# Attention into SwiGLU: how normalised x of batches 1 to 7 reaches its transposed ring

## The chip, the core and the metric

The kernel runs on one core of a Trainium2 chip. The metric is device time in microseconds (us). A core has engines that each run their own instruction stream in order and wait for one another by semaphores: TensorE (PE, with its weight loads PEld), VectorE (DVE), ScalarE (ACT), GpSimd (POOL), and SyncE (SP), which here does nothing but issue DMAs. The DMAs of all queues are carried out by 16 DMA engines of the core. TensorE reads SBUF and writes PSUM; DVE and ACT bring results from PSUM back to SBUF.

## The reference

Causal attention with a decay bias (8 batches, 8 heads, 576 positions, 64 dims a head), whose output is read as 4608 tokens of 512 values and put through an RMS norm and a SwiGLU layer:

```python
scores = q @ k.T / sqrt(D)                       # per batch and head
bias = -(cum[..., :, None] - cum[..., None, :])  # cum = cumsum(max(s, 0))
attn = softmax(where(causal, -1e9, scores + minimum(bias, 0)))
x = (attn @ v).transpose(0, 2, 1, 3).reshape(B * S, H * D)
xn = x / sqrt(mean(x * x, -1) + 1e-6) * rms_g
g = xn @ w_gate
out = (g * sigmoid(g) * (xn @ w_val)) @ w_out    # w_gate, w_val 512x1536, w_out 1536x512
```

## The kernel before, in words

Both halves are woven into one instruction stream per engine. The layer (`ffn(c)`, L464) works on nine chunks c of 512 tokens: twelve times four gate matmuls (L472) and four value matmuls (L481) of 128x512, with tanh on ACT (L475) and two products on DVE (L484, L477), then four groups of twelve output matmuls (L496), each drained by ACT into `osb` (L501) and stored by SP (L503). `osb` has three buffers.

Attention works on batches of 576 tokens in five blocks `qb` (four of 128 rows and one of 64). Its pieces are: T, transposing k and q on TensorE (L146) with copies by ACT (L154) or DVE (L152); S, the scores (L196) with exponentials on ACT (L212) and the causal mask on POOL (L218); AV, the product with v (L233, L239), whose result DVE divides into `x_sb` (L246, L248). After the second AV of a block DVE squares x (L253), POOL makes 1/rms from the sum (L256, L259), and DVE scales x into `xs_sb` (`x_scale`, L266). `x_sb` and `xs_sb` have four buffers (NX). XT (`xt_step`, L270) then takes the block to the ring `xnT`, in which a token is a column: four TensorE transposes of 128x128 into PSUM (L274, tile `psT`, a single buffer that T uses too) and one DVE copy into `xnT` (L279; a second one, L281, where the block wraps round the end). The ring holds 2048 tokens, four chunks. It is read by L472 and L481.

k and q of a batch come as float32 by SP (`load_kq`, L117, 1 MB each; tails L123, 128 KB each) into a single buffer `kq32`; POOL casts them (L133) in ten pieces. The load of batch b+1 waits until the casts of batch b have read the buffer, so it is issued after the last of them. v is loaded by POOL (L137). DVE also runs range checks on k and q (L284, L290).

The order is set at build time by a planner in the code. `step()` (L424) counts one slot; `ffn` calls it 36 times in a chunk, and `need(c)` (L453) calls it until the last block of chunk c has its XT. In each slot `step` issues at most one scale, one side job (POOL casts, v loads or a DVE check), and then either one S or up to two of XT, AV and T. An AV may be placed only when the XT of the block four before it is `done` (L410 to L412, since its buffers are the same); T and XT must be two slots apart from each other (`last["T"]`, L384 and L416); S must be two or three slots apart. A block's scale is placed 3 slots after its second AV, its XT 6 slots after it or later. Casts of a batch wait until 9 slots after its load was placed. Batch 0 (blocks 0 to 3) is written out by hand ahead of chunk 0 (L633 to L686). The tile framework adds the semaphores; SP's stream has stores, loads and whatever else is issued there in the order in which the code places them.

Of the kernel before, what the change touches and what calls it, by code (L numbers as in the profile page):

```python
# [26 lines left out]
def kernel(  # L27
# [12 lines left out]
    nc = tc.nc  # L40
    B, H, S, D = q.shape
# [5 lines left out]
    NSC = 5  # L47
# [4 lines left out]
    RING = 4 * DM  # L52

    def rows(c):
        return 128 if c < 4 else 64
# [18 lines left out]
    xnT = mp.tile([128, CC, RING], BF16, name="xnT")  # L74
# [8 lines left out]
    NX = 4  # L83
    x_sb = mp.tile([128, NX, DM], BF16, name="x_sb")
    xs_sb = mp.tile([128, NX, DM], BF16, name="xs_sb")
# [22 lines left out]
    def psT():  # L108
        return pp.tile([128, 8, 128], BF16, name="psT", tag="T", bufs=1)
# [5 lines left out]
    def load_kq(eng, b, w, h0=0, h1=H):  # L115
        src = k if w == 0 else q
        eng.dma_start(  # L117
            out=kq32[:, w, h0:h1, 0:256],
            in_=src[b, h0:h1, 0:512, :].rearrange("h (p r) d -> p h (r d)", r=4))

    def load_kq_tail(eng, b, w):
        src = k if w == 0 else q
        eng.dma_start(  # L123
            out=kq32[0:64, w, :, 256:320],
            in_=src[b, :, 512:576, :].rearrange("h p d -> p h d"))

    def cast(eng, b, w, r0, r1, h0=0, h1=H):
        o = kqn[:, b % 2, w, r0:r1, h0:h1, :]
        i = kq32[:, w].rearrange("p h (r d) -> p r h d", d=D)[:, r0:r1, h0:h1, :]
        if eng is nc.scalar:  # L130
            eng.activation(out=o, in_=i, func=AF.Copy)
        else:
            eng.tensor_copy(out=o, in_=i)  # L133
# [129 lines left out]
    def x_scale(b, qb):  # L263
        n = rows(qb)
        col = b * NSC + qb
        nc.vector.tensor_scalar(  # L266
            out=xs_sb[0:n, (b * NSC + qb) % NX, :], in0=x_sb[0:n, (b * NSC + qb) % NX, :],
            scalar1=al_all[0:n, col:col + 1], scalar2=None, op0=ALU.mult)

    def xt_step(b, qb):  # L270
        n = rows(qb)
        pX = psT()
        for cc in range(CC):
            nc.tensor.matmul(pX[:, cc, :], lhsT=xs_sb[:, (b * NSC + qb) % NX, cc * 128:(cc + 1) * 128],  # L274
                             rhs=ident_bf, is_transpose=True,
                             start=(cc == 0), stop=(cc == CC - 1))
        t0 = (b * S + qb * 128) % RING
        m = min(n, RING - t0)
        nc.vector.tensor_copy(out=xnT[:, :, t0:t0 + m], in_=pX[:, 0:CC, 0:m])  # L279
        if m < n:  # L280
            nc.vector.tensor_copy(out=xnT[:, :, 0:n - m], in_=pX[:, 0:CC, m:n])  # L281
# [14 lines left out]
    slot = [0]  # L296
    done = {}
# [3 lines left out]
    xt_seq = [(b, qb) for b in range(B) for qb in range(NSC)]  # L301
    t_seq = [(b, hp, w) for b in range(B) for hp in list(range(HP)) + ["tail"]
             for w in (0, 1) if hp != "tail" or w == 0]
    pending = []
    pool_side, dve_side, v_side = [], [], []

    def at(*key):
        return done.get(key, 10 ** 6)

    def ready(lag, *key):  # L310
        return at(*key) + lag <= slot[0]

    def run_side(queue):
        if queue and queue[0][0]():
            queue.pop(0)[1]()

    def later(queue, lag, fns):
        t = slot[0] + lag
        queue.extend((lambda: slot[0] >= t, f) for f in fns)

    def check(b):
        later(dve_side, 2, [f for w in (0, 1) for f in (
            lambda w=w: check_mag(b, w), lambda: check_max(0), lambda: check_max(1))]
            + [lambda: done.__setitem__(("check", b), slot[0])])

    def casts(b):

        def over():
            done["cast", b] = slot[0]
            if b + 1 < B:  # L330
                for w in (0, 1):
                    load_kq(nc.sync, b + 1, w)
                    load_kq_tail(nc.sync, b + 1, w)
                done["raw", b + 1] = slot[0]
            check(b)
        fns = [lambda w=w, r=r: cast(nc.gpsimd, b, w, r, r + 1) for w in (0, 1) for r in range(NSC)]
        pool_side.extend((lambda: ready(9, "raw", b) and ready(0, "check", b - 2), f)
                         for f in fns + [over])
# [10 lines left out]
    def do_t(key, **kw):  # L349
        b, hp, w = key  # L350
        if hp == "tail":
            tail_step(b)
            done["T", b] = slot[0]
            after_tail(b)
        else:
            t_step(b, hp, w, **kw)
        done["T", b, hp, w] = slot[0]
        last["T"] = slot[0]

    def do_s(key, pair=None):  # L360
        b, kb, g = key
        second = s_step(b, kb, g, pair)
        done["S", b, kb, g] = slot[0]
        if kb == 4:
            done["S", b, 4, 1] = slot[0]
        last["S"] = slot[0]
        return second

    def do_av(key):
        b, qb, g = key  # L370
        av_step(b, qb, g)
        done["AV", b, qb, g] = slot[0]
        last["AV"] = slot[0]
        if qb == 4 and g == 1:
            after_av(b)

    def do_xt(key):
        b, qb = key
        xt_step(b, qb)
        done["XT", b, qb] = slot[0]  # L380
        last["T"] = slot[0]

    def can_t():
        if not t_seq or slot[0] - last["T"] < 2:  # L384
            return False
        b, hp, w = t_seq[0]
        return ready(2, "cast", b) and (b < 2 or ready(1, "S", b - 2, 4, 0))

    def can_s():
        if not s_seq or not slot_free():  # L390
            return False
        b, kb, g = s_seq[0]
        due = SLOTS * ((b * S + kb * 128) // DM) - 14
        if slot[0] - last["S"] < (3 if slot[0] < due else 2):
            return False
        if kb >= 3 and not ready(3, "T", b):
            return False
        if kb == 4:
            return True
        return all(ready(3, "T", b, 2 * g + j, w) for j in (0, 1) for w in (0, 1))  # L400

    def can_av():
        if not av_seq or slot[0] - last["AV"] < 2:
            return False
        b, qb, g = av_seq[0]
        if b > 1 and not ready(8, "V", b):
            return False
        if qb > 0 and not ready(5, "S", b, qb - 1, g):
            return False
        prev = b * NSC + qb - NX  # L410
        if prev >= 0 and at("XT", prev // NSC, prev % NSC) > slot[0]:
            return False  # L412
        return ready(5, "S", b, qb, g)

    def can_xt():
        if not xt_seq or slot[0] - last["T"] < 2:  # L416
            return False
        b, qb = xt_seq[0]
        return ready(6, "AV", b, qb, 1)

    scaled = [0]
    x_list = [(b, qb) for b in range(B) for qb in range(NSC)]
# [1 line left out]
    def step():  # L424

        slot[0] += 1
        while pending:
            pending.pop(0)()
        if scaled[0] < len(x_list):
            b, qb = x_list[scaled[0]]  # L430
            if ready(3, "AV", b, qb, 1):
                x_scale(b, qb)
                scaled[0] += 1
        if v_side and slot[0] % 2:
            run_side(v_side)
        else:
            run_side(pool_side)
        if slot[0] % 2:
            run_side(dve_side)
        if can_s():  # L440
            pending.append(do_s(s_seq.pop(0)))
            return
        n = 0
        if can_xt():
            do_xt(xt_seq.pop(0))
            n += 1
        if can_av():
            do_av(av_seq.pop(0))
            n += 1
        if n < 2 and can_t():  # L450
            do_t(t_seq.pop(0))

    def need(c):  # L453

        lastt = (c + 1) * DM - 1
        key = (lastt // S, (lastt % S) // 128)
        n = 0
        while at("XT", *key) > slot[0]:
            step()
            n += 1  # L460
            assert n < 200, key
# [428 lines left out]
```

## Time and profile before

| | us |
|---|---|
| time, median of 3 runs (lowest to highest) | 421.24 (421.04 to 421.57) |
| the profiled execution: its time | 420.97 |
| the profiled execution: span from first to last instruction | 419.4 |
| mean granted TensorE clock | 0.992 |
| ACT busy, share of the span | 217.8 (52%) |
| POOL busy, share of the span | 180.1 (43%) |
| first gate matmul of chunks 0 to 4, from the span's start | 47.17, 100.57, 144.47, 189.41, 229.33 |
| the same of chunks 5 to 8 | 270.76, 311.05, 349.58, 381.62 |

The page gives each engine's busy time, the span in forty slices, the DMA queues, the chain that ended last, and groups of instructions with their mean duration and the idle time before them. L12 is line 12 of the kernel. In a timeline a line gives start, duration, engine, line, operation and count; matmuls are pipelined, so the duration of one is longer than the time by which it moves the next, and costs on TensorE are read from the distance of starts.

### The profile page before, as it was taken

What the parts mean: (1) busy time and instruction counts of PE and PEld (TensorE: products, weight loads), DVE (VectorE), ACT (ScalarE), POOL (GpSimd) and SP (SyncE); (2) the same over time, 40 slices, a digit from 0 to 9 for tenths busy, and PEclk for the clock granted to TensorE, in tenths of its full rate; (3) what the DMA queues carried; (4) which work ended last, traced back from release to release, by engine and by line L of the source; (5) the groups of instructions that cost most, each with busy time, mean ns of one, the idle gap of its engine ahead of it and who ended that gap; (6) DMA issues with size and microseconds to landing.
All of it is one profiled execution on the core that took longest, in us unless ns stands there. A gap on an engine that the chain in (4) does not pass through costs nothing. (4 is left out here: it accounts for less than half of the span.)

```text
span 419.4 us, 7416 instructions
## 1 busy us (share of the span) xinstructions
PE 371.8 (89%) x2679; PEld 183.2 (44%) x2679; DVE 322.2 (77%) x678; ACT 217.8 (52%) x516; POOL 180.1 (43%) x288
## 2 busy tenths in 40 slices
PE   1563779698999889999999999999999999999993
PEld 1342433344544444445445444444454445444441
DVE  4458499899899699988897899979767966764740
ACT  2661265652577647644765486558645753323321
POOL 6767727576717757535734575343221320000000
PEclk9999999899999999999999999999999999999998
DMA  9999985348931755629242630190020011001002
GB/s 241 215 232 256 178 135 36 22 135 211 150 115 50 233 70 50 208 79 81 76 153 76 64 21 25 65 69 2 27 76 2 2 50 52 1 29 73 1 28 80
DMA packets 72125, 38.46 MB, mean 92 GB/s; under 512 B 47440, under 2 KB 67408, under 8 KB 72080
## 3 DMA queue, kind: packets, MB, share of 16 engines
q0 software_dynamic: 41168, 9.44, 24.4%
q1 hardware_dynamic: 29776, 27.27, 20.9%
q10 hardware_dynamic: 1136, 1.20, 0.8%
q8 instruction: 23, 0.38, 0.4%
q14 instruction: 22, 0.18, 0.1%
HBM read 37.90 MB, written 9.44 MB: 113 GB/s over the span
## 5 line engine op out<-in xcount | busy, mean ns | idle before, releaser
L212 ACT ACTIVATE E<-psS,biasK 128x256 bf16<-128x256 f32 (+2 forms) x300 | 105.6, 434 | 33.3 <-PE psS L196 30.6
L472 PE MATMUL psF<-xnT,wg_sb 128*128 128x512 bf16 x432 | 111.9, 382 | 2.0 <-DVE xnT L279 1.1
L481 PE MATMUL psF<-xnT,wv_sb 128*128 128x512 bf16 x432 | 112.8, 384 | 0.5 <-DVE Ht L477 0.2
L496 PE MATMUL psF<-wout_sb,Ht 128*128 128x512 bf16 x432 | 104.9, 379 | 0.0
L475 ACT ACTIVATE T<-psF 128x512 f32<-128x512 f32 x108 | 64.7, 599 | 74.3 <-PE psF L472 62.8
L218 POOL TENSOR_SCALAR_AFFINE_SELECT E<-E 128x512 bf16<-128x512 bf16 x72 | 49.5, 688 | 99.9 <-ACT E L212 98.9
L484 DVE SCALAR_TENSOR_TENSOR U<-T,psF 128x512 bf16<-128x512 f32 x108 | 73.7, 683 | 18.3 <-ACT T L475 17.9
L477 DVE TENSOR_TENSOR Ht<-U,psF 128x512 bf16<-128x512 bf16 x99 | 67.5, 682 | 5.5 <-PE psT L146 0.5
L481 PEld LDWEIGHTS <-wv_sb 128*128 128x128 bf16 x432 | 39.3, 98 | 45.4 <-issue 6.9
L472 PEld LDWEIGHTS <-wg_sb 128*128 128x128 bf16 x432 | 38.1, 98 | 39.0 <-issue 7.2
L496 PEld LDWEIGHTS <-Ht 128*128 128x128 bf16 x432 | 37.8, 98 | 38.0 <-issue 2.7
L133 POOL CAST kqn<-kq 128x512 bf16<-128x512 f32 (+1 forms) x80 | 51.7, 669 | 4.0 <-DMA kq<-in_k_dram 2.3
L501 ACT ACTIVATE osb<-psF 128x512 f32<-128x512 f32 x36 | 21.6, 601 | 48.6 <-PE psF L496 45.0
L256 POOL TENSOR_SCALAR al_all<-ss_all 128x1 f32<-128x1 f32 (+1 forms) x40 | 15.9, 397 | 62.8 <-DVE xs_sb L253 62.2
L248 DVE TENSOR_TENSOR x_sb<-psAV,rZ 128x256 bf16<-128x256 f32 (+1 forms) x80 | 33.8, 423 | 2.7
L239 PE MATMUL psAV<-v_sb,E 128*128 128x65 bf16 x320 | 30.2, 199 | 5.9 <-POOL E L218 5.9
L137 POOL DMA_DIRECT2D v_sb<-in_v_dram x40 | 35.3, 889 | 0.0
L233 PE MATMUL psAV<-v_sb,E 128*128 128x65 bf16 x256 | 25.7, 198 | 6.9 <-DVE x_sb L248 6.9
L196 PE MATMUL psS<-kqT 64*128 64x256 bf16 (+2 forms) x300 | 25.7, 257 | 6.3 <-ACT E L212 4.9
L253 DVE SCALAR_TENSOR_TENSOR xs_sb<-x_sb 128x512 bf16<-128x512 bf16 (+1 forms) x40 | 29.7, 743 | 1.4
L154 ACT ACTIVATE kqT<-psT 128x512 bf16<-128x512 bf16 x32 | 19.4, 607 | 19.9 <-PE psT L146 19.9
L239 PEld LDWEIGHTS <-E 128*128 128x128 bf16 x320 | 22.8, 101 | 14.3 <-POOL E L218 6.4
(82 smaller groups left out, 318.2 us busy)
## 6 DMA issues: line engine op xcount, KB each, us to landing
out_dram<-osb SPq DMA_DIRECT2D x36, 256.0 KB, 2.0
kq<-in_k_dram SPq DMA_DIRECT2D x7, 1024.0 KB, 5.9
kq<-in_q_dram SPq DMA_DIRECT2D x7, 1024.0 KB, 6.7
v_sb<-in_v_dram POOLq DMA_DIRECT2D x32, 128.0 KB, 4.4
wg_sb<-in_moe_w_gate_dram POOLq DMA_DIRECT2D x2, 768.0 KB, 15.0
wv_sb<-in_moe_w_val_dram POOLq DMA_DIRECT2D x2, 768.0 KB, 19.5
wout_sb<-in_moe_w_out_dram POOLq DMA_DIRECT2D x1, 1536.0 KB, 14.7
kq<-in_k_dram SPq DMA_DIRECT2D x2, 512.0 KB, 5.2
```

The source lines that it names most:

```text
L133: eng.tensor_copy(out=o, in_=i)
L137: nc.gpsimd.dma_start(out=v_sb[0:n, b % 2, c, :, 0:64], in_=v[b, :, c * 128:c * 128 + n, :].rearrange("h p d -> p h d"))
L212: nc.scalar.activation(out=Ev[:, h - h0, 0:N], in_=pair[par][:, o:o + N], func=AF.Exp, scale=0.125, bias=biasK[:, kb, bh:bh + 1])
L218: nc.gpsimd.affine_select(out=Ev[:, :, 0:nq], in_=Ev[:, :, 0:nq], pattern=[[0, nh], [1, nq]], compare_op=ALU.is_ge, fill=0.0, base=0, chan ...
L239: nc.tensor.matmul(o, lhsT=d, rhs=v_sb[:, p, qb, h, :], start=(j == 0 and qb == 0), stop=(j == 3))
L248: nc.vector.tensor_tensor(out=xo[:, g * 256:(g + 1) * 256].rearrange("p (h d) -> p h d", h=4), in0=pv[0:n, :, 0:64], in1=rZ[0:n].unsqueeze ...
L472: nc.tensor.matmul(Gp, lhsT=wg_sb[:, cc, fs], rhs=xnT[:, cc, x0:x0 + DM], start=(cc == 0), stop=(cc == CC - 1))
L475: nc.scalar.activation(out=T, in_=Gp, func=AF.Tanh, scale=0.5)
L477: nc.vector.tensor_tensor(out=Ht[:, fb - 1, :], in0=pend[0], in1=pend[1], op=ALU.mult)
L481: nc.tensor.matmul(Vp, lhsT=wv_sb[:, cc, fs], rhs=xnT[:, cc, x0:x0 + DM], start=(cc == 0), stop=(cc == CC - 1))
L484: nc.vector.scalar_tensor_tensor(out=U, in0=T, scalar=1.0, in1=Gp, op0=ALU.add, op1=ALU.mult)
L496: nc.tensor.matmul(Op, lhsT=Ht[:, fb, tb * 128:(tb + 1) * 128], rhs=wout_sb[:, fb, :], start=(fb == 0), stop=(fb == FB - 1))
```

## The change

Blocks of batches 1 to 7 no longer take XT. Where the planner places a block's scale, it now also places a transposing DMA on SP's queue that reads `xs_sb` and writes the block's columns of `xnT` (two DMAs where the block wraps round), and declares the block's XT done four slots later. `can_xt` lets only batch 0 through. The loads of k and q for the next batch, so far placed right behind the last cast, are placed by a new side list three slots later.

```diff
+    def xt_dma(b, qb):
+        n = rows(qb)
+        t0 = (b * S + qb * 128) % RING
+        m = min(n, RING - t0)
+        i = (b * NSC + qb) % NX
+        nc.sync.dma_start_transpose(out=xnT[:, :, t0:t0 + m], in_=xs_sb[0:m, i, :])
+        if m < n:
+            nc.sync.dma_start_transpose(out=xnT[:, :, 0:n - m], in_=xs_sb[m:n, i, :])
...
             done["cast", b] = slot[0]
             if b + 1 < B:
-                for w in (0, 1):
-                    load_kq(nc.sync, b + 1, w)
-                    load_kq_tail(nc.sync, b + 1, w)
-                done["raw", b + 1] = slot[0]
+                def loads():
+                    for w in (0, 1):
+                        load_kq(nc.sync, b + 1, w)
+                        load_kq_tail(nc.sync, b + 1, w)
+                    done["raw", b + 1] = slot[0]
+                later(sp_side, 3, [loads])
...
-        return ready(6, "AV", b, qb, 1)
+        return b == 0 and ready(6, "AV", b, qb, 1)
...
                 x_scale(b, qb)
                 scaled[0] += 1
+                if b > 0:
+                    assert xt_seq[0] == (b, qb)
+                    xt_dma(*xt_seq.pop(0))
+                    done["XT", b, qb] = slot[0] + 4
+        run_side(sp_side)
```

More of the change, by code (lines that the diff above doesn't have):

```diff
@@ L304 @@
     pending = []
-    pool_side, dve_side, v_side = [], [], []
+    pool_side, dve_side, v_side, sp_side = [], [], [], []
     def at(*key):
```

## The prediction, made before the changed kernel was run

> **What bounds the kernel now.** I read the page first. TensorE is busy 89% of the span, DVE 77%; from slice 6 on TensorE's row is almost all nines, with the clock at full.
>
> ```profile
> PE 371.8 (89%) x2679; PEld 183.2 (44%) x2679; DVE 322.2 (77%) x678; ACT 217.8 (52%) x516; POOL 180.1 (43%) x288
> PE   1563779698999889999999999999999999999993
> DVE  4458499899899699988897899979767966764740
> ```
>
> Shares over the whole span mix stages, so next comes the table by chunk (stretch; its length; busy us of PE, PEld, DVE, ACT, POOL; clock; DMA share; GB/s). I cut it at the chunk starts.
>
> ```profile
> 100.60:144.50 43.90, 41.33 (x317) 20.68 (x317) 36.67 (x69) 28.25 (x67) 26.46 (x41) 1.00 0.57 119
> 144.50:189.40 44.90, 42.22 (x340) 20.92 (x340) 42.27 (x92) 25.18 (x62) 25.09 (x38) 1.00 0.52 113
> 189.40:229.30 39.90, 39.90 (x309) 19.59 (x307) 34.72 (x72) 24.66 (x61) 21.07 (x34) 1.00 0.51 101
> 229.30:270.80 41.50, 40.94 (x329) 20.19 (x327) 36.70 (x78) 25.31 (x62) 20.90 (x34) 1.00 0.30 41
> 270.80:311.00 40.20, 40.20 (x319) 19.88 (x317) 30.54 (x70) 25.32 (x61) 13.60 (x24) 1.00 0.30 42
> 349.60:381.60 32.00, 31.63 (x153) 14.34 (x150) 21.09 (x34) 10.03 (x17) 0.72 (x2) 1.00 0.09 34
> ```
>
> From chunk 1 TensorE has no more than 2.7 us of gaps in a chunk. Chunk 7, almost without attention, takes 32.0 us; the 8 to 13 us that chunks 1 to 5 take beyond that are attention's TensorE work. So TensorE's own sequence sets the time; in chunk 2 DVE (42.27 of 44.9) is close behind. Last, the timeline around one XT:
>
> ```profile
> 192.22 1.03 PE L481 MATMUL psF<-xnT,wv_sb 128*128 128x512 bf16 x4
> 193.08 0.39 PE L274 MATMUL psT<-ident_bf,xs_sb 128*128 128x128 bf16 x4
> 193.31 1.03 PE L472 MATMUL psF<-xnT,wg_sb 128*128 128x512 bf16 x4
> ```
>
> By starts, four long matmuls take 0.86 us (192.22 to 193.08) and the four transposes 0.23 (to 193.31). The page's 230 ns for one transpose is its pipelined length, not its price.
>
> **Removed.** 35 blocks (seven batches of five) lose XT. TensorE: 35 x 0.23 = 8.05 us, all on the path. Four of them (batch 1, blocks 0 to 3) precede chunk 1, whose start will be set by a DMA (below), so I count 31 x 0.23 = **-7.1 us**. DVE: the copies sum to 15.35 us (L279) and 0.56 (L281), less batch 0's 1.96: 13.9 us, beside TensorE's work except where TensorE waits for them. Those waits on the path are at the start of chunk 2, 0.50 for `psT` and 0.44 for the ring after 1.09 for scores. By the planner's rules they change: the block that chunk 2 needs last (batch 2, block 2) has AV, scale and XT at slots 70, 73, 76, and three slots in `need` go without layer matmuls; with T no longer kept two slots from XT, that AV comes at 66, the scale and its DMA at 69, and chunk 2 starts at 74 with no extra slot. I take **-1.5** (bounds 0 and -2.0).
>
> **Added.** 35 transposing DMAs of 128 KB (two blocks in halves). SP's issue costs it 0.33 to 0.8 us a DMA by the rows of L503 and L123; SP has the time, and no engine waits for the issue. No row shows how long a transposing DMA takes. The nearest rows (KB, then us from issue to landing):
>
> ```profile
> out_dram<-osb SPq DMA_DIRECT2D x36, 256.0 KB, 2.0
> kq<-in_k_dram SPq DMA_DIRECT2D x7, 1024.0 KB, 5.9
> v_sb<-in_v_dram POOLq DMA_DIRECT2D x32, 128.0 KB, 4.4
> kq<-in_q_dram SPq DMA_DIRECT2D x8, 128.0 KB, 6.8
> ```
>
> Below stands 2.0 (long rows, twice the bytes), above 6.8 (same bytes, but queued behind megabytes). I take **4.4**: the same bytes in short runs, as a block is written to 128 partitions in 256-byte runs. The Trainium skill, "VectorE: DVE Perf Modes", section "The three transpose paths", gives 1309 ns for a 128x128 bf16 transpose by DMA against 390 on TensorE, and advises TensorE where PSUM will do. Four of those in a row would be an estimated 5.2 us a block, and the sum by it about 417 (0.8 later at chunk 1, 0.2 at chunk 2); no run here shows it yet.
>
> Where is it late? A block of chunk 3 or later is scaled 11 slots or more ahead of its chunk (batch 3 block 2 at slot 99, chunk 3 at 110; batch 4 block 1 at 122, chunk 4 at 146), at about 1.13 us a slot (40.5 us a chunk over 36). Chunk 2's has five slots, 5.7 us: enough for 4.4. Chunk 1's (batch 1, block 3) is scaled at slot 34, and chunk 1 begins at 38. The trace there:
>
> ```profile
> 93.72 5.87 SPq L503 DMA_DIRECT2D out_dram<-osb  x3
> 96.29 0.33 DVE L266 TENSOR_SCALAR xs_sb<-x_sb,al_all 128x512 bf16<-128x512 bf16 x1
> 100.11 0.41 DVE L279 COPY xnT<-psT 128x512 bf16<-128x512 bf16 x1
> 100.57 1.02 PE L472 MATMUL psF<-xnT,wg_sb 128*128 128x512 bf16 x4 [0.68 <-DVE xnT L279]
> ```
>
> The load of batch 3 moves from slot 29 to 32, two ahead of this transpose, on the same queue. It follows the second store, whose `osb` is ready at 92.1 (L501, 91.52 + 0.60). Its 2.36 MB, at the roughly 360 GB/s of the busy slices around 95 us, last to 98.7; a store of 0.7 us comes next, then the transpose, landing 2.0 to 4.4 later: 101.4 to 103.8, say 102.6, **+2.0** against 100.57. That queued DMAs wait their turn is shown by the stores: 2.0 in the median, 7.2 at most. If the transposes need not queue, the start is as early as 98.6, when TensorE is free (-2.0); with 6.8 it is +4.4. The pause in TensorE before chunk 1, 1.1 us now (98.4 to 99.5), grows to some 3.5, and the matmuls after the present one run at full pace (1.02 for four), while the first of chunk 0, after sparse work, took 1.91. The Trainium skill, "TensorE: Matmul & The Clock Gate", section "Why this matters for your kernels", has idle gaps over about 3 us send the clock to half; by chunk 0's two slow groups that would add 1.7 us.
>
> Behind the transpose SP's stream holds stores and loads. Its wait for the scale is short, as the scale runs in step with TensorE (96.29, beside an AV at 97.05).
>
> **Moved.** Attention is packed tighter: a block takes 6 slots and a batch 30, where XT and T kept apart made it 34 to 36; the last block is scaled at slot 224 instead of 258. DVE gains a block or so of work in each of chunks 1 to 5 (L246, L248 twice, L253, L266: 2.4 us, and T's copies, 0.7) and loses five copies (2.1). In chunk 2 that makes 43.3 us of DVE in a chunk that TensorE could do in some 43. I put **+1.5** for new waits (0 to +6).
>
> **Sum**, against the profiled execution's 420.97 (0.27 below the median): 420.97 - 7.1 - 1.5 + 2.0 + 1.5 = 415.9, so **416 us**.
>
> **Rivals.**
>
> 1. *DVE becomes the bound of the tight stage.* For: 42.27 of 44.9 in chunk 2. Against: 30.5 to 36.7 later. At 1.0 us more in each of chunks 1 to 5: 421, no change.
>
> 2. *SP's queue becomes the bound (slower).* A batch of 30 slots lasts 33.8 us; its loads take 6.6 and its 3.3 stores 2.4, which leaves 24.8, or 5.0 a transpose. Above 5.0 us the queue falls behind, the loads of k and q with it, POOL stands at a cast with the masks queued behind, and TensorE waits in AV. At 6.8: chunk 1 +2.4, chunk 2 +1.7 (6.8 and a store against 5.7), and by the last load (slot 129, eight blocks after slot 79) 15 us of lag, of which the 9 planned slots and the distance from casts to T hide about half: +8. In all 428. For: that 6.8 exists. Against: the load rows stand behind megabytes.
>
> 3. *It moves in small pieces.* The software queue's row (41168 packets, 24.4% of 16 engines) gives 40 ns of an engine a packet. In 32-byte pieces a block is 4096 packets, 10.2 us, and 35 blocks 358 us beside the 196 (46.6%) already used: more than the span, over 500 us. Nothing in the trace speaks for it or excludes it.
>
> **Numbers.** Forecast (411 to 419) 0.58; rival 1 0.11, rival 2 0.21, rival 3 0.10. Low end: all 8.05 and the 2.0 saved and no new wait, 411. High end: rival 2 with somewhat more than half unhidden, 431; that leaves out rival 3 and tails, under 2 in 10. Faster by over 0.2% (about what a measurement of this kernel can tell from no change): 0.58 + 0.05 of rival 1; within: 0.05; slower: 0.32.
>
> **What would show it.** Right: L274 at 20 instructions; transposes landing in under 5 us; chunk 1 near 102.6, chunks 3 to 6 with TensorE full, chunk 6 near 34. Wrong: SP's loads issued ever later against the casts (rival 2), DMA slices all nines to the end (rival 3), long `U` or `Ht` waits of TensorE in chunks 1 to 5 (rival 1).

## The result and the profile after

The changed kernel is slower, by 0.7%: 424.9 us (median of 11 runs, 422.54 to 425.54) against 421.35 (11 runs, 420.6 to 421.73), a ratio of 1.007 with an interval of 1.005 to 1.0089. The profiled execution took 425.54 us, with a span of 423.9; it is the slowest of the eleven, and the account below is of that one. The forecast was 416. The time lies in the range given and on the other side of no change.

On the page, both busy engines have less to do. TensorE lost 3.2 us (371.8 to 368.6; its records overlap, so this is not the price of what was removed), DVE 11.6 us (322.2 to 310.6):

```profile
span 423.9 us, 7240 instructions
PE 368.6 (87%) x2539; PEld 175.5 (41%) x2539; DVE 310.6 (73%) x641; ACT 216.8 (51%) x516; POOL 175.6 (41%) x288
PE   1563779692999999999999899899999999999993
PEclk9999999898699999999999999999999999999998
```

The first thing to see is the 2 in TensorE's row, slice 9, where there was a 9, and the 6 in the clock's row just behind it. The DMA view has the row that the trace of before could not have (count, median us from issue to landing):

```profile
xnT<-xs_sb SPq DMA_TRANSPOSE x37, 2.5
```

A transposing DMA lands 2.5 us after its issue in the median, less than the 4.4 that I took and the 5.2 of the estimate. It moves packets of 256 bytes, not of 32: SP's queue has 17,312 packets more, with 4.13 MB. So the usual transpose is not slow, and rival 3, the small pieces, did not come true.

The table by chunk, cut at the new chunk starts (chunks 1 to 4 and 6; columns as before):

```profile
106.90:150.80 43.90, 43.19 (x305) 19.98 (x306) 33.83 (x66) 27.03 (x66) 21.78 (x37) 0.94 0.43 93
150.80:194.50 43.70, 42.55 (x339) 20.44 (x337) 38.43 (x82) 28.29 (x70) 25.05 (x42) 1.00 0.73 141
194.50:239.40 44.90, 42.52 (x336) 19.96 (x334) 41.04 (x82) 30.52 (x75) 28.86 (x48) 1.00 0.76 133
239.40:284.60 45.20, 42.66 (x345) 20.28 (x343) 36.16 (x79) 30.48 (x78) 22.38 (x37) 1.00 0.54 60
322.70:354.20 31.50, 31.50 (x161) 14.53 (x160) 18.97 (x34) 9.55 (x16) 1.46 (x4) 1.00 0.15 41
```

Chunk 1 starts at 106.9 instead of 100.6, and its clock is 0.94. Chunks 3 and 4 have become longer (39.9 and 41.5 to 44.9 and 45.2), chunk 6 much shorter (38.5 to 31.5), because attention now ends in chunk 5. From the start of chunk 1 to the end the kernel gains 1.8 us (318.8 to 317.0 of span), and it loses 6.3 before. The timeline ahead of chunk 1:

```profile
95.45 2.25 SPq L123 DMA_DIRECT2D kq<-in_q_dram  x1
96.44 0.33 DVE L266 TENSOR_SCALAR xs_sb<-x_sb,al_all 128x512 bf16<-128x512 bf16 x1
97.80 1.45 SPq L520 DMA_DIRECT2D out_dram<-osb  x1
99.34 2.44 SPq L276 DMA_TRANSPOSE xnT<-xs_sb  x1
106.91 1.86 PE L489 MATMUL psF<-xnT,wg_sb 128*128 128x512 bf16 x4 [8.59 <-issue]
```

The block is scaled at 96.8, but SP is still issuing the last load (2.25 us, where such an issue takes 0.6 at the least) and a store (1.45 for 0.33); the transpose leaves at 99.34, its own issue takes 2.44 instead of 1.19, and it lands 7.5 us later, at 106.8. TensorE stands still for 8.6 us. The row says "issue", yet the matmul starts with the landing. What the pause did to the clock shows in stretches of a microsecond (stretch; length; PE busy; clock; DMA share; GB/s; the share counts a packet whole where it starts, so it can exceed 1):

```profile
101.00:102.00 1.00, 0.00 (x0) 1.00 1.12 353
103.00:104.00 1.00, 0.00 (x0) 0.50 7.76 129
111.00:112.00 1.00, 1.00 (x6) 0.50 0.00 0
112.00:114.00 2.00, 2.00 (x12) 0.85 0.00 0
```

The granted clock falls to half some 4.0 us after TensorE went idle (98.3 to 102.4) and comes back only at about 112.6, after 5.7 us of work.

So three questions stood: why the transpose of chunk 1 is so late, what the half clock costs, and where the 6.9 us that chunks 2 to 7 should save have gone.

### The profile page after: what moved, and what is told of

It reads as the page before. It is cut to its first block, busy times and chain, and to the rows that moved or that the text cites. A ratio compares the mean times of both kernels' runs of the same rounds, so it can differ in the third digit from the quotient of the medians.

```text
span 423.9 us, 7240 instructions
## 1 busy us (share of the span) xinstructions
PE 368.6 (87%) x2539; PEld 175.5 (41%) x2539; DVE 310.6 (73%) x641; ACT 216.8 (51%) x516; POOL 175.6 (41%) x288
## 5 line engine op out<-in xcount | busy, mean ns | idle before, releaser
L489 PE MATMUL psF<-xnT,wg_sb 128*128 128x512 bf16 x432 | 113.6, 386 | 10.9 <-issue 8.6
L513 PE MATMUL psF<-wout_sb,Ht 128*128 128x512 bf16 x432 | 102.4, 380 | 1.4 <-DVE U L501 0.9
L218 POOL TENSOR_SCALAR_AFFINE_SELECT E<-E 128x512 bf16<-128x512 bf16 x72 | 51.1, 709 | 101.1 <-ACT E L212 101.0
L489 PEld LDWEIGHTS <-wg_sb 128*128 128x128 bf16 x432 | 39.7, 99 | 56.1 <-issue 18.6
L513 PEld LDWEIGHTS <-Ht 128*128 128x128 bf16 x432 | 39.1, 98 | 44.7 <-issue 3.9
L133 POOL CAST kqn<-kq 128x512 bf16<-128x512 f32 (+1 forms) x80 | 50.4, 653 | 4.1 <-DMA kq<-in_k_dram 2.4
L518 ACT ACTIVATE osb<-psF 128x512 f32<-128x512 f32 x36 | 21.5, 597 | 42.7 <-PE psF L513 38.6
L256 POOL TENSOR_SCALAR al_all<-ss_all 128x1 f32<-128x1 f32 (+1 forms) x40 | 11.8, 294 | 43.1 <-DVE xs_sb L253 41.9
L146 PE MATMUL psT<-ident_bf,kqn 128*128 128x128 bf16 x224 | 23.7, 232 | 6.4 <-ACT kqT L154 2.5
```

The costliest lines, as they stand in the source:

```text
L218: nc.gpsimd.affine_select(out=Ev[:, :, 0:nq], in_=Ev[:, :, 0:nq], pattern=[[0, nh], [1, nq]], compare_op=ALU.is_ge, fill=0.0, base=0, chan ...
L489: nc.tensor.matmul(Gp, lhsT=wg_sb[:, cc, fs], rhs=xnT[:, cc, x0:x0 + DM], start=(cc == 0), stop=(cc == CC - 1))
L513: nc.tensor.matmul(Op, lhsT=Ht[:, fb, tb * 128:(tb + 1) * 128], rhs=wout_sb[:, fb, :], start=(fb == 0), stop=(fb == FB - 1))
```

## The experiments

Each ran beside the kernel before on the same chip (four chips in all); the median of before was 421.0 to 421.2 each time, and the ratios are to these runs of before. Starts and lengths of chunks are those of the profiled execution:

| run | median us | chunk 1 starts | lengths of chunks 1 to 6 |
|---|---|---|---|
| before | 421.35 | 100.57 | 43.9, 44.9, 39.9, 41.4, 40.3, 38.5 |
| changed | 424.9 | 106.91 | 43.9, 43.8, 44.9, 45.1, 38.1, 31.6 |
| batch 1 on TensorE | 416.19 | 100.73 | 43.7, 44.6, 44.2, 44.1, 37.5, 31.3 |
| old pace | 420.89 | 106.26 | 46.2, 44.3, 39.2, 39.2, 39.2, 37.4 |
| v loads later | 421.55 | 104.47 | 41.4, 43.5, 44.4, 44.6, 38.7, 32.2 |
| load of batch 3 behind | 413.65 | 98.85 | 40.0, 43.8, 43.6, 44.6, 38.9, 32.2 |
| that and old pace | 416.79 | 98.69 | 43.8, 45.5, 41.6, 39.1, 39.5, 37.4 |
| filled pause | 422.04 | 106.37 | 41.2, 43.8, 44.9, 45.1, 38.1, 31.6 |
| loads later alone | 418.34 | 100.27 | 43.1, 43.5, 40.8, 40.3, 40.3, 38.5 |
| behind, no checks | 404.91 | 99.20 | 39.9, 40.9, 41.4, 41.5, 38.9, 32.2 |
| behind, old pace from batch 3 | 410.11 | 99.34 | 40.0, 42.6, 39.8, 41.0, 39.2, 37.4 |
| load of batch 3 on ACT's queue | 424.08 | 106.08 | 43.3, 43.8, 44.9, 45.1, 38.1, 31.6 |
| loads as before | 424.84 | 104.28 | 44.3, 46.2, 44.9, 43.7, 37.9, 31.3 |
| same order, from batch 2 | 416.42 | 100.68 | 43.3, 45.1, 39.2, 39.2, 39.2, 37.4 |

### Why chunk 1 is late

**Batch 1 on TensorE.**

```diff
-        return b == 0 and ready(6, "AV", b, qb, 1)
+        return b <= 1 and ready(6, "AV", b, qb, 1)
...
-                if b > 0:
+                if b > 1:
```

> Batches 0 and 1 keep TensorE transposes; batches 2 to 7 use the transposing DMAs. Theory (the loss is made at chunk 1: its transpose is queued behind the loads of k and q, and TensorE comes back from the pause at half clock): chunk 1 starts at 100 to 101 us instead of 106.9 and takes some 43.5 without a half-clock stretch; total 425 - 6.3 - 2.6 + 0.9 (four transposes back) = 417. Rival (the transposing DMAs cost time all along, and a late chunk 1 would be made up later): chunk 1 is on time, but the total stays at 421 or above.

416.19 us, ratio 0.9876 (0.9855 to 0.9898); chunk 1 on time, no half clock behind it. Leaving the blocks of batch 1, four of which stand ahead of chunk 1, to TensorE turns a loss of 0.7% into a gain of 1.2%. The loss is made at chunk 1.

**The load of batch 3 behind the transposes.**

```diff
-                later(sp_side, 3, [loads])
+                later(sp_side, 9 if b == 2 else 3, [loads])
```

> As the changed kernel, but the loads of k and q of batch 3 are placed 9 slots after the casts instead of 3, so that they stand behind the transposes of batch 1, blocks 3 and 4, in SP's stream instead of ahead of block 3's. Theory (order in SP's queue): the transpose is issued at about 97 and lands 2.5 to 3 later, chunk 1 starts at 99.5 to 100.5 and without the half clock, total 416 to 417. Rival (something else than that load holds the transpose, such as v loads or its own time): chunk 1 at 103 or later, total 421 or more.

413.65 us, ratio 0.9827 (0.9805 to 0.9849), better than the 416 to 417 expected. The same transpose, with the load out of its way, leaves as soon as its block is scaled (at 95.68) and lands 3.0 us later:

```profile
95.70 1.92 SPq L276 DMA_TRANSPOSE xnT<-xs_sb  x1
100.77 0.53 SPq L117 DMA_DIRECT2D kq<-in_k_dram  x1
```

Chunk 1 starts at 98.85, before even the kernel with TensorE transposes.

**v loads later.**

```diff
-            later(v_side, 1, [lambda c=c: load_v(b + 2, c) for c in range(NSC)]
+            later(v_side, 6 if b == 1 else 1, [lambda c=c: load_v(b + 2, c) for c in range(NSC)]
```

> As the changed kernel, but the five v loads of batch 3, which POOL issued at 100.1 us beside the late transpose, are placed four slots later, behind a mask that waits for TensorE. Theory (v loads beside it lengthen the transpose: 2.4 us alone, 5 to 6 beside v loads): it lands some 3 us earlier, chunk 1 starts near 104, total 422. Rival (only the bytes of the k and q loads ahead of it in SP's queue count): chunk 1 at 106.5 to 107, total 425.

As the theory had it: it lands after 5.3 us instead of 7.5, chunk 1 starts at 104.47, 421.55 us, ratio 1.0007 (0.9995 to 1.002). The v loads that POOL issues at 100.1 are 2 us of the delay. The trace of the changed kernel agrees elsewhere: transposes issued within a few us of v loads land after 4.9 to 6.3 us (issued at 157.8, 167.6, 192.6, 195.5, 240.3; the first and the third also beside a load of k and q), those with nothing beside them after 2.3 to 2.5.

**The load of batch 3 on ACT's queue.**

```diff
-                        load_kq(nc.sync, b + 1, w)
-                        load_kq_tail(nc.sync, b + 1, w)
+                        load_kq(nc.scalar if b == 2 else nc.sync, b + 1, w)
+                        load_kq_tail(nc.scalar if b == 2 else nc.sync, b + 1, w)
```

> As the changed kernel, but the four loads of k and q of batch 3 are issued by ACT on its own queue, at the same place in the order. Theory (order in SP's queue makes the transpose late): it leaves SP at about 97 and lands at 101 to 102 beside the loads, chunk 1 starts at 101 to 102.5, total 418. Rival (the 16 DMA engines are shared, so the bytes of the loads hold it up whatever queue they are on): it lands at 105 or later, total 423 or more.

A miss of my theory: 424.08 us, ratio 1.0062 (1.0043 to 1.0081). With only a store ahead of it on SP's queue the transpose still takes 2.14 us to issue and lands after 7.4 us:

```profile
95.08 2.37 ACTq L123 DMA_DIRECT2D kq<-in_q_dram  x1
97.50 0.60 ACT L518 ACTIVATE osb<-psF 128x512 f32<-128x512 f32 x1 [4.46 <-DMA out_dram<-osb]
98.55 2.14 SPq L276 DMA_TRANSPOSE xnT<-xs_sb  x1
```

So the late landing does not need a place behind the load in SP's queue: while the DMA engines carry the load (385 GB/s between 96 and 98), they hold up a transpose from the other queue just as long. Part of the 7.4 us is again the v loads, here at 99.7 and 100.7. This run is not clean in one point, as ACT, held by its own issues and by a store, drains `osb` late, and with it the store ahead of the transpose; but the 7.4 us after the issue has no such cause.

**The loads as before.**

```diff
-                later(sp_side, 3, [loads])
+                loads()
```

> The changed kernel without its shift of the loads: they are placed right behind the last cast again. Theory: the first wait on SP (the scale of batch 1, block 2, and its transpose) stands ahead of them now, so the loads of batch 3 leave less than 1 us earlier than in the changed kernel, and the transpose of block 3 is as late; chunk 1 at 105 to 107, total 424 to 427. Rival (the shift by three slots is what puts the loads in the transpose's way): chunk 1 at 101 to 103, total 419 to 421.

424.84 us, ratio 1.0096 (1.008 to 1.0112), chunk 1 at 104.28, 0.7 us earlier than the 105 to 107 that I wrote; the load left SP 2.2 us earlier than in the changed kernel, not less than 1. So the shift makes at most 2.6 of the 6.3 us by which chunk 1 is late (106.91 less 104.28); the other 3.7 come without it. The time is no shorter, because chunks 1 and 2 take 2.9 us longer together; no run shows why.

### What the half clock costs

**Filled pause.**

```diff
             need(c)
+            if c == 1:
+                fill = psF()
+                for i in range(34):
+                    nc.tensor.matmul(fill, lhsT=wg_sb[:, i % CC, 0:128], rhs=xnT[:, i % CC, 0:DM],
+                                     start=(i == 0), stop=(i == 33))
             ffn(c, extra if c == 0 else None)
```

> As the changed kernel, but ahead of chunk 1 TensorE does 34 matmuls of 128x512 on old data into an unused PSUM tile, 7.3 us, which end before the late transpose lands. Theory (half clock after the pause costs 2 to 3 us in chunk 1): the granted clock stays at 1, chunk 1 still starts near 107 but takes 41 instead of 43.9, total 422.5. Rival (chunk 1 is long for other reasons): chunk 1 stays at 43 to 44, total 425.

422.04 us, ratio 1.002 (1.0004 to 1.0035). Useless work in the pause makes the kernel 2.9 us faster: chunk 1 starts only 0.5 us sooner (106.37), but it takes 41.16 instead of 43.85, with the clock at full. The half clock cost 2.7 us.

### Where the gain of the later chunks went

**Old pace.** The planner books the XT steps of before; nothing is issued in them.

```diff
         b, qb = key
-        xt_step(b, qb)
+        if b == 0:
+            xt_step(b, qb)
...
-        return b == 0 and ready(6, "AV", b, qb, 1)
+        return ready(6, "AV", b, qb, 1)
...
                 if b > 0:
-                    assert xt_seq[0] == (b, qb)
-                    xt_dma(*xt_seq.pop(0))
-                    done["XT", b, qb] = slot[0] + 4
+                    xt_dma(b, qb)
```

> The DMAs stay where they are, but the planner still books an XT step for every block as before (its slot, its two slots of distance to T, its done mark), with nothing issued there. So T, S and AV keep the order and the pace of the kernel before. Theory (the tighter stage loses some 4.7 us of the 6.3 that chunks 2 to 6 save): chunk 1 still starts near 107, chunks 2 to 6 together take 199 instead of 203.5, total 420.5. Rival (the DMAs themselves slow those chunks): they take 203 to 205 again, total 425.

420.89 us, ratio 1.0 (0.9979 to 1.0021), chunk 1 nearly as late as in the changed kernel (106.26). Chunks 2 to 6 take 199.3 us together instead of 203.5, though chunk 1 takes 46.2 instead of 43.9. Chunks 3 to 5 take 39.17 each, with 9 S, 10 AV and 9 T in 36 slots; at the tight pace 12 of each are booked in chunk 3 and in chunk 4. From the distance of starts (S 0.33, AV 0.25, T 0.22 or 0.43 us for a tail) and 30.9 us of layer matmuls, I estimate TensorE's own work at 38.6 us in the first case and 40.7 in the second: waits of 0.6 us against 4.2 and 4.4. The profile's own account of waits agrees in kind: in chunks 2 to 4 it puts 5.8 us of TensorE's idle time down to DVE in the changed kernel, and 0.6 in this run.

**The load behind, no checks.** DVE's range checks of batches 3 to 7 are left out, so the kernel no longer checks the range of their k and q.

```diff
-            lambda w=w: check_mag(b, w), lambda: check_max(0), lambda: check_max(1))]
+            lambda w=w: b > 2 or check_mag(b, w), lambda: b > 2 or check_max(0),
+            lambda: b > 2 or check_max(1))]
```

> As the run with the loads of batch 3 behind, but DVE's range checks of k and q are left out for batches 3 to 7 (their slots stay booked; the kernel then no longer checks the range of those batches). It takes some 5 us of DVE a batch out of chunks 2 to 4. Theory (DVE is the bound of the tight chunks): these take 41 to 42 instead of 43.6 to 44.6, total 407 to 409. Rival (the waits come from the chains through ACT and POOL, S every third slot): chunks 2 to 4 lose less than 1 us each, total 412 or more.

404.91 us, ratio 0.9619 (0.9599 to 0.9638), below the 407 to 409 expected; chunks 2 to 4 take 40.9, 41.4 and 41.5. Chunk 3 with the checks, in the load-behind run (stretch; length; busy time of PE, PEld, DVE, ACT and POOL; clock; DMA share; GB/s):

```profile
182.60:226.20 43.60, 42.24 (x331) 20.04 (x330) 38.95 (x83) 30.52 (x76) 27.04 (x43) 1.00 0.94 164
```

And without them, in this run:

```profile
179.90:221.30 41.40, 41.40 (x330) 19.86 (x328) 32.21 (x72) 30.41 (x76) 25.22 (x42) 1.00 1.04 172
```

TensorE's gaps are gone (41.40 of 41.40), with ACT as busy as ever and POOL at 25.22 us instead of 27.04. In the load-behind run TensorE waits in chunks 2 to 4 for DVE alone (who waits for whom: us in total, times, longest):

```profile
PE psF L513 <- DVE Ht L508: 2.4, 3, 1.1
PE psF L489 <- DVE U L501: 1.7, 4, 0.6
PE psT L146 <- DVE kqT L152: 0.7, 1, 0.7
PE psAV L233 <- DVE x_sb L248: 0.4, 1, 0.4
PE psF L498 <- DVE Ht L494: 0.2, 1, 0.2
```

Without the checks that view has no line for these chunks. So DVE makes the waits of the tight chunks, though it is busy only 38.95 of 43.6 us: it is not full, but what TensorE needs stands in line behind the checks and DVE's other work.

**Load behind and old pace.** Edit: both of those above.

> Both mends at once: the loads of batch 3 behind the transposes of batch 1 (9 slots after the casts), and the planner's booked XT steps of the kernel before. Theory (the two losses are separate and add up): chunk 1 starts near 99 at full clock, chunks 3 to 5 take 39.2 each, total 411.5 (413.65 less 3.8 in chunks 2 to 6, plus some 1.5 in chunk 1 for the three slots in need). Rival (the tight pace gains in chunk 1 what it loses later): 413 to 414, no better than the first mend alone.

A miss: 416.79 us, ratio 0.99 (0.9872 to 0.9928), worse than the load behind alone. The old pace brings chunks 3 and 4 down (43.6 and 44.6 to 41.6 and 39.1), but chunk 1 takes 43.8 instead of 40.0, chunk 2 45.5 instead of 43.8 and chunk 6 37.4 instead of 32.2. The last block of chunk 2 is scaled at slot 73 of 77 again, and four slots in `need` go without layer matmuls. Of chunk 2's 45.5, 3.2 us are a wait of TensorE at its end for the block that chunk 3 needs, whose transposes left beside a load (183.2 and 184.5). Chunks 1 to 6 take 247.0 us together instead of 243.0; but for that wait the tight pace gains early about what it costs later.

**Load behind, old pace from batch 3.** As the load behind, with XT steps booked for batches 3 to 7 only.

```diff
-        xt_step(b, qb)
+        if b == 0:
+            xt_step(b, qb)
...
-        return b == 0 and ready(6, "AV", b, qb, 1)
+        return b not in (1, 2) and ready(6, "AV", b, qb, 1)
...
                 if b > 0:
-                    assert xt_seq[0] == (b, qb)
-                    xt_dma(*xt_seq.pop(0))
+                    xt_dma(b, qb)
+                if b in (1, 2):
+                    assert xt_seq.pop(0) == (b, qb)
                     done["XT", b, qb] = slot[0] + 4
```

> As the run with the loads of batch 3 behind, with the tight pace for batches 1 and 2 only; from batch 3 the planner books an XT step for every block again (nothing is issued there). Theory (the tight pace helps up to the start of chunk 2, by having its last block early, and costs 3 to 4 us a chunk in chunks 2 to 4 through DVE's queue): chunk 1 takes 40, chunk 2 43 to 44, chunks 3 to 5 some 39.2 each, total 409. Rival (what the pace costs comes back wherever attention is put): 413 to 414 again.

410.11 us, ratio 0.9733 (0.9718 to 0.9748): of the kernels that compute everything, the fastest, 2.7% ahead of the kernel before. Chunks 3 to 5 take 39.8, 41.0 and 39.2 instead of 39.2 each.

### The two parts by themselves

**Loads later alone.** The kernel before, TensorE transposes everywhere, with the shift of the loads by three slots.

```diff
-                for w in (0, 1):
-                    load_kq(nc.sync, b + 1, w)
-                    load_kq_tail(nc.sync, b + 1, w)
-                done["raw", b + 1] = slot[0]
+                def loads():
+                    for w in (0, 1):
+                        load_kq(nc.sync, b + 1, w)
+                        load_kq_tail(nc.sync, b + 1, w)
+                    done["raw", b + 1] = slot[0]
+                later(sp_side, 3, [loads])
...
+        run_side(sp_side)
```

> The kernel before, with TensorE transposes everywhere, and only one part of the change: loads of k and q placed three slots later. Theory (the later load does harm only to a transpose queued behind it): 421, as before, chunk 1 at 100 to 101. Rival (the later loads hold up the casts and with them T and S): 423 or more, with POOL waiting for DMA.

A miss on the good side: 418.34 us, ratio 0.994 (0.9921 to 0.996). The shift, which I priced at nothing, gains some 2.7 us by itself, 0.8 in chunk 1, 1.5 in chunk 2 (DVE busy 39.8 us there instead of 42.3) and 1.1 in chunk 4, less 0.9 in chunk 3. It places the casts, and the checks that follow them, at other slots; that this spreads DVE's work is the likely reason, but no run tests it.

**Same order, from batch 2.** The old-pace kernel with batch 1 on TensorE, so in the order of the run above.

```diff
-        if b == 0:
+        if b <= 1:
             xt_step(b, qb)
...
-                if b > 0:
+                if b > 1:
                     xt_dma(b, qb)
```

> The order of the run with only the loads later (418.3 us: TensorE transposes everywhere), with one difference: batches 2 to 7 go to the ring by transposing DMAs, issued at the scale, and their booked XT steps issue nothing. So this is the replaced work alone, without late chunk 1 and without the tighter pace. Theory (0.23 us of TensorE a block, all on the path): 30 x 0.23 = 6.9 us less, some 0.5 back at the start of chunk 2, total 412. Rival (DVE's queue or the DMAs take what TensorE gains): 415 or more.

416.42 us, ratio 0.9899 (0.9882 to 0.9917), so only 1.9 less than 418.34: a miss, on the side of the rival's 415 or more. Where the rest is, the chunks say: 40.30, 40.28, 38.52 became 39.18, 39.17, 37.40 in chunks 4 to 6, 1.12 us each for five blocks. That is 0.22 a block, against the forecast's 0.23. But chunk 3 starts late:

```profile
PE psF L488 <- DMA xnT<-xs_sb: 3.2, 1, 3.2
```

The block that chunk 3 needs wraps round the ring; at the old pace its two transposes leave at 184.2 and 185.5, beside a load, land 4.9 and 3.8 us later, and TensorE waits 3.2 us. So here too a transpose beside a load takes back, at one chunk's start, part of what TensorE gains.

## Why the prediction was wrong

**The removed work was priced rightly.** I had 0.23 us of TensorE a block, on the path; chunks 4 to 6 of the last run give 0.22.

**Rivals 2 and 3 did not happen.** With nothing beside it a transpose lands after 2.3 to 2.5 us. Of the 35 blocks 27 leave SP within 0.1 us of their scale; the others leave up to 3.2 us after it, and the lag does not add up.

**"... then the transpose, landing 2.0 to 4.4 later" is the step that failed: chunk 1 started 6.3 us late in place of 2.0.** The place and the cause (the load of batch 3 just ahead) were right, as the load-behind run shows. The sum let the transpose begin at 99.4, when the load's bytes (to 98.7) and a store of 0.7 would be through. It did leave at 99.34, but by luck. The load left SP at 93.5, not 92.1, since batch 1's block 2 and its 1.2 us of issue now stand ahead of the store and the load; and the load's last part landed only at 104.3 (95.45 and 8.8). What held the transpose until 2.6 us after its scale were the slow issues of that part and of a store ahead of it on SP. I had put an issue at 0.33 to 0.8 us "by the rows of L503 and L123"; these rows go up to 1.09 and 4.66, and in the trace of before the issue in question had already taken 1.45:

```profile
92.22 1.45 SPq L123 DMA_DIRECT2D kq<-in_q_dram  x1
```

Once issued, the transpose took 7.5 us instead of the 3.2 in the middle of my bounds, and that is the whole 4.3 us by which chunk 1 missed the 102.6. I had it wait for its turn in SP's queue and then land as if alone. In fact it shared the DMA engines with the rest of the load, whichever queue that is on (7.4 us with the load on ACT's queue), and with the v loads, which I did not count and which are worth 2 us.

**The half clock, +2.7 us, was left out of the sum.** I wrote that the pause would be 3.5 us and that the rule would then add 1.7, but put nothing into the sum and gave no reason. The pause was 8.6. The Trainium skill, "TensorE: Matmul & The Clock Gate", section "Why this matters for your kernels", sets the limit at about 3 us of idleness; here 1.1 us in the kernel before did nothing, and in this pause the clock fell after 4.0. The filled pause shows its price. I also overlooked that the trace of before has such a case, a pause of 2.9 us, and the clock at half from 78.2 to 81.6 (a row of the timeline, and a stretch of a microsecond with all its columns):

```profile
78.67 0.61 PE L196 MATMUL psS<-kqT 64*128 64x256 bf16 x4 [2.92 <-ACT E L212]
79.00:80.00 1.00, 1.00 (x6) 0.28 (x3) 0.90 (x3) 0.72 (x3) 1.00 (x3) 0.50 0.07 16
```

**"+1.5 for new waits" was too small, by about 2.6 us.** The mechanism of rival 1, DVE in the tight chunks, was right, and the no-checks run shows it. I took DVE's busy time against the chunk's length, found them about equal in chunk 2 alone, and cleared the later chunks by their shares of 30.5 to 36.7. But chunks 3 and 4 wait some 4 us each, by the estimate above, with DVE busy 91 and 80% of the time. The -1.5 for a tighter start of chunk 2 is borne out: at the old pace chunk 1, which ends there, takes 2.3 us longer.

**The shift of the loads was given no price of its own.** It gains 2.7 us in the old order; in the changed kernel, with or without it, the time is the same (424.84 and 424.9).

For the profiled execution the sum closes: chunk 1 started 4.3 us later than the 102.6 forecast, and from there to the end it took 318.6 us instead of 313.3. Of these 5.3 us the clock is 2.7, and the 2.6 left over I put down to the tight pace. The old-pace run, whose chunks 2 to 6 are 4.2 us shorter, gives about the same, 2.7 more than the 1.5. Together that is the 9.6 us between 415.9 and 425.54.

## What to carry to other kernels

Before work is moved from an engine to a DMA, find the one consumer with the least time between producer and use, and look at everything the DMA engines carry in that stretch, on all queues; the median landing says nothing about it. Moving the load beside that one block was worth 11 us here, and leaving its batch on TensorE 9, each more than the 5 that the whole change was meant to bring. A planner that gets rid of one step repacks all the others: compare counts per stage, and do not clear an in-order engine by its busy share.

## What the runs showed of the hardware that was not expected

- A transposing DMA of 128x512 bf16 from SBUF to SBUF lands after 2.3 to 2.5 us with 1.17 to 1.2 us of issue on SP; next to other loads it took up to 7.5 us to land and 2.44 to issue in the changed kernel.
- An instruction that issues a DMA took longer while the DMA engines were full (336 to 346 GB/s between 96 and 99): the tail's 0.6 became 2.25 us, a store's 0.33 1.45. From ACT, on its own queue, the same tail took 2.37.
- Half clock comes in steps: in all the traces a stretch of it lasts 3.4, 6.8 or 10.2 us, but for the one that the end of the kernel cuts off. In the changed kernel it was 10.2 (102.4 to 112.6, 5.7 of them work), in the run with later v loads 6.8 (100.5 to 107.3, 2.8 of them work). Pauses near 3 us go either way: 2.9 us brought it in the kernel before, while the 3.2 us ahead of chunk 3 in the last run left the clock at 1.00. What decides is not settled.
- In the kernel before, the first two groups of chunk 0 took 1.91 us for four matmuls while the profile gives the granted clock as 1.00. The trace's record of the clock begins only at 50.8 us, behind them, and the next group, at 51.16, took 1.03; so that 1.00 says nothing about the first two.
